# Attention and GELU MLP on one core: seven products of blocks instead of eight for the first product of the last two tiles

## The chip, the cores and the metric

The kernel runs on one core of a Trainium2 chip. The metric is the device time of one execution in microseconds (us), the median of several runs. The engines of the core that matter here are TensorE (PE in the profile; its weight loads are shown apart, as PEld), VectorE (DVE), ScalarE (ACT), GpSimd (POOL), and SyncE (SP), whose queue issues every DMA of this kernel.

## What is computed

For 8 batches of 8 heads with 576 positions of 64 numbers: causal attention in a window of 128 positions with a linear bias for each head, and then an MLP with GELU on the 4608 rows of 512 that it leaves. Cut to what matters:

```python
scores = scale * q @ k.T                      # for each batch and head
scores = where(mask, scores + bias, -1e9)     # 0 <= i - j < 128, bias = -slope * (i - j)
attn = softmax(scores) @ v
x = attn as [4608, 512]
h = x @ w_in                                  # 512 -> 2048
g = 0.5 * h * (1 + erf(h / sqrt(2)))
out = g @ w_out                               # 2048 -> 512
```

## The kernel before

Every large operand of a product is held as two fp16 parts, a high one and a low one, after a scaling by a power of two, and a product of two such operands takes three matmuls: high by high, low by high, high by low. The parts are made by ACT or POOL (high) and DVE (low, `low_part`, L146).

The 4608 rows of x are worked in nine tiles of 512 (t = 0 to 8). A tile has two products. The first, `mlp_in` (L588 to L620), takes 16 blocks fc of 128 columns of w_in; each is 4 parts of the contraction by 3 terms, 12 matmuls of 512 columns (L595), so 192 in a tile. ACT takes each block out of PSUM with Gelu (L618) into a tile of the tag `ob` (three buffers), POOL makes the high part (L619), DVE the low part (L146). The second, `mlp_out` (L638), takes 4 blocks tb of 128 rows, 16 fc by 3 terms each, again 192 matmuls of 512 columns (L653); DVE or ACT takes the result out (L663, L661) and SP stores it (L664). Both products share four PSUM banks (tag `mm`). The weights of w_in stay in eight pairs `wi[n]`, [128, 2 parts, 4 parts of the contraction, 256 columns].

Attention of batch b = t + 1 is issued in the middle of tile t, for t up to 6, so tiles 7 and 8 hold the MLP alone. A batch has four units hp. Of each: the scores on PE (L410, tile `sc`, PSUM tag `att`), taken out by DVE with the bias (L432, tile `s`), a maximum on DVE (L502, `nmax`), exponentials on ACT (L505), the split into `e_main` by POOL (L514) and DVE (L146), two transposes by DMA into `et` (L517: EVEN, five groups, then ODD, four), and the product with v on PE (`weigh`, L554, tile `av`), taken out into the rows of x of the next tiles (L567 on ACT, then L146). Beside them run the steps for the next batch: `load_v`, `stat_v` (L214 is its maximum over all of v, `stv`), `split_v` (`vbuf`), `load_qk`, `split_qk` (`qbuf`, `kbuf`).

The program writes these in the order of steps in the loop at L767: step 0 to 15 issues `mlp_in`, step 16 to 31 four fc of `mlp_out`, scores at `SCORES_AT`, weighings at `WEIGH_AT`. From that a scheduler with a timeline of its own and priorities sets the order of each engine; an engine then runs its list strictly in order. So an instruction that waits holds back all behind it on its engine, and a DMA that waits holds back all behind it on SP. The exponentials are given a higher priority (`EXP_AHEAD`).

## Time and profile before

| | us |
|---|---|
| median of 3 runs (lowest to highest) | 954.64 (951.97 to 955.38) |
| the profiled execution | 956.14 |
| its span in the trace | 954.3 |
| PE busy | 920.4 |
| DVE busy | 626.1 |
| ACT busy | 493.4 |
| POOL busy | 214.5 |
| mean granted clock of TensorE | 0.984 of full speed |

The profiled execution took 956.14 us, of which the trace covers a span of 954.3; the 1.8 us between them lie outside the instructions. A sum made on the trace is a sum against 956.14, which is 1.5 us above the median of the runs. [...]

### The profile page before, as it was taken

What the parts mean: (1) busy time and instruction counts of PE and PEld (TensorE: products, weight loads), DVE (VectorE), ACT (ScalarE), POOL (GpSimd) and SP (SyncE); (2) the same over time, 40 slices, a digit from 0 to 9 for tenths busy, and PEclk for the clock granted to TensorE, in tenths of its full rate; (3) what the DMA queues carried; (4) which work ended last, traced back from release to release, by engine and by line L of the source; (5) the groups of instructions that cost most, each with busy time, mean ns of one, the idle gap of its engine ahead of it and who ended that gap; (6) DMA issues with size and microseconds to landing.
All of it is one profiled execution on the core that took longest, in us unless ns stands there. A gap on an engine that the chain in (4) does not pass through costs nothing.

```text
span 954.3 us, 17680 instructions
## 1 busy us (share of the span) xinstructions
PE 920.4 (96%) x7068; PEld 448.8 (47%) x7068; DVE 626.1 (66%) x1270; ACT 493.4 (52%) x1071; POOL 214.5 (22%) x444
## 2 busy tenths in 40 slices
...
DVE  6799989689786877497768876777566722201200
...
DMA packets 172450, 91.18 MB, mean 96 GB/s; under 512 B 132560, under 2 KB 153168, under 8 KB 172240
## 3 DMA queue, kind: packets, MB, share of 16 engines
...
q14 instruction: 27, 0.22, 0.1%
...
## 4 chain that ended last, share of the span: by engine, by line
PE 54%; DMA 2%; DVE 2%; ACT 2%; issue 1%; SPq 0%; POOL 0%; DVEq 0%
PE o L653 26%; PE h L595 22%; PE av L554 3%; PE sc L410 2%; DMA v<-vp 1%; DMA q<-qp 1%; DVE stv L214 1%; DMA et<-e_main 1%; ACT vbuf L332 1%; DVE vbuf L146 0%; ACT s L505 0%; DVE kbuf L146 0%; ACT L618 0%; ACT L505 0%; SPq L305 0%
## 5 line engine op out<-in xcount | busy, mean ns | idle before, releaser
L595 PE MATMUL h<-x,wi 128*128 128x512 f16 x1728 | 385.0, 381 | 6.6 <-ACT g L618 3.0
L653 PE MATMUL o<-wo,g 128*128 128x512 f16 x1224 | 276.4, 379 | 0.2 <-DVE wo L146 0.2
L595 PEld LDWEIGHTS <-wi 128*128 128x128 f16 x1728 | 166.8, 98 | 209.2 <-issue 12.3
L653 PEld LDWEIGHTS <-g 128*128 128x128 f16 x1632 | 155.0, 98 | 186.6 <-issue 2.3
L146 DVE SCALAR_TENSOR_TENSOR g<-g,sg,g 128x512 f16<-128x512 f32 (+1 forms) x144 | 114.1, 805 | 92.7 <-POOL g L619 91.5
L619 POOL TENSOR_SCALAR g<-g,sg 128x512 f16<-128x512 f32 x128 | 100.4, 788 | 316.7 <-ACT g L618 312.4
L505 ACT ACTIVATE s<-s,nmax 128x192 f32<-128x192 f32 x252 | 111.2, 442 | 103.2 <-DVE nmax L502 103.0
L618 ACT ACTIVATE g<-h,gs 128x512 f32<-128x512 f32 x128 | 85.9, 687 | 135.8 <-PE h L595 111.0
L146 DVE SCALAR_TENSOR_TENSOR e_main<-s,z,e_main 128x192 f16<-128x192 f32 x252 | 107.3, 468 | 15.0 <-POOL e_main L514 10.2
L514 POOL TENSOR_SCALAR e_main<-s,z 128x192 f16<-128x192 f32 x180 | 87.1, 503 | 84.9 <-ACT s L505 29.3
L653 PE MATMUL o<-wo_first,g 128*128 128x512 f16 x408 | 94.6, 382 | 2.8 <-DMA wo_first<-wo 2.8
L410 PE MATMUL sc<-kbuf,qbuf 64*64 64x192 f16 (+1 forms) x1656 | 75.6, 264 | 10.8 <-DMA kbuf<-kp 4.5
L432 DVE SCALAR_TENSOR_TENSOR s<-sc,cs,bias_h 128x384 f32<-128x384 f32 x112 | 63.7, 606 | 14.3 <-PE sc L410 14.1
L567 ACT ACTIVATE x<-av,cx 128x448 f16<-128x448 f32 (+6 forms) x52 | 23.7, 474 | 72.8 <-PE av L554 72.6
L437 POOL MEMSET s<- 64x128 f32 (+1 forms) x112 | 19.2, 172 | 185.8 <-DVE s L432 167.3
L502 DVE TENSOR_REDUCE nmax<-s 128x5 f32<-128x960 f32 (+1 forms) x56 | 58.4, 1044 | 2.1
L661 ACT ACTIVATE ob<-o,so 128x512 f32<-128x512 f32 x17 | 11.5, 678 | 91.2 <-PE o L653 91.1
L410 PEld LDWEIGHTS <-qbuf 64*64 64x64 f16 x1512 | 36.1, 106 | 43.0 <-issue 40.2
L663 DVE TENSOR_SCALAR ob<-o,so 128x512 f32<-128x512 f32 x17 | 12.6, 744 | 60.0 <-PE o L653 60.0
L554 PEld LDWEIGHTS <-vbuf 128*64 128x64 f16 x1680 | 43.3, 115 | 12.4 <-issue 11.5
L554 PE MATMUL av<-et,vbuf 128*64 128x128 f16 (+1 forms) x1680 | 46.4, 216 | 2.6 <-DMA et<-e_main 2.6
L505 ACT ACTIVATION_READ_ACCUMULATOR s<-s,nmax 128x1 f32 x252 | 47.1, 187 | 0.0
...
## 6 DMA issues: line engine op xcount, KB each, us to landing
...
out<-ob SPq DMA_DIRECT2D x36, 256.0 KB, 2.1
...
```

The source lines that it names most:

```text
L146: nc.vector.scalar_tensor_tensor(out=dst, in0=src, scalar=scale, in1=high, op0=ALU.mult, op1=ALU.subtract)
L410: nc.tensor.matmul(ps[bank][o, n, 0:W], a, m, start=(i == 0), stop=(i == len(terms) - 1 and b > 0), skip_group_check=True,)
L432: nc.vector.scalar_tensor_tensor(out=s[:, bank[0] : bank[0] + k, :], in0=ps[bank][:, 0:k, 0:W], scalar=cs, in1=bias.broadcast_to([P, k, W] ...
L502: nc.vector.tensor_reduce(out=nmax[:, r], in_=s[:, r], axis=AX.X, op=ALU.max, negate=True)
L505: nc.scalar.activation(s[:, i, :], s[:, i, :], AF.Exp, bias=nmax[:, i : i + 1], accum_out=z[:, i : i + 1])
L514: nc.gpsimd.tensor_scalar(e[:, i, 0, c], s[:, i], z[:, i : i + 1], 1.0, op0=ALU.mult, op1=ALU.mult)
L554: nc.tensor.matmul(av[r, (j - blocks[0]) * QB : (j - blocks[0] + len(js)) * QB], v32s[b][:, hp, kb, r] if b < EXACT else vbuf[:, vi, hp, k ...
L567: nc.scalar.activation(x[:, 0], av[:, :n], AF.Copy, scale=c)
L595: nc.tensor.matmul(ph, wi[n][:, a, cc, k * P : (k + 1) * P], x[:, cc, b, :], start=(i == 0), stop=(i == 3 * NCC - 1),)
L618: nc.scalar.activation(g32, ph, AF.Gelu, scale=gsc[t, n])
L619: nc.gpsimd.tensor_scalar(g[:, r, 0], g32, gsg[t, n], 1.0, op0=ALU.mult, op1=ALU.mult)
L653: nc.tensor.matmul(o, both[:, a, c], wo[n][:, b, k, :], start=(fc == first and i == 0), stop=(fc == last and i == 2),)
```

## The change

**Tiles 7 and 8 (`FAST = 7`).** The first product is made in four groups d of 512 columns of w_in (two pairs `wi`). In each, the weights are four blocks (256 columns by half of the contraction) and x is four blocks (half of the contraction by 256 rows), and the eight products of blocks are replaced by seven (p1 to p7) of sums of blocks. Each is 2 by 2 by 3 = 12 matmuls of 256 columns, so a group has 84 and a tile 336. Two PSUM banks, u and v, gather them; ACT copies u to SBUF three times in a group (s1, s2, s3), DVE adds v to these copies, and four results of [128, 512] go through Gelu on ACT, a high part on ACT (before: POOL) and a low part on DVE. That is 11 ACT and 7 DVE instructions in a group. `p4` and `p3` of the last group are issued in the second product.

**Sums of weights.** Four sums of blocks (T1 to T4) are needed for each d. They are made once, in 16 parts of [128, 512] (`sums_of_weights`): two additions of 256 on DVE, four dependent ones of 128, a cast on ACT, a difference of 512 on DVE, and four DMAs that store them to DRAM in pieces of 256 bytes. Three parts each stand beside the second products of tiles 2 to 5, four beside that of tile 6. T1 is then loaded over a block of `wi[2d + 1]` that is no longer needed (four DMAs); T2 to T4 are loaded for each d as they are needed, 256 KB each, into one buffer each (`stream`), the next one behind the product that reads the last.

**Sums of x.** `sums_of_x` makes the sums of blocks of x: six DVE instructions (two of 1024, four of 256) and a cast of 1024 on ACT, twice for a tile: for tile 7 in tile 6, behind the weighings of units 1 and 3, for tile 8 in the second product of tile 7.

**Smaller things.** One power of two is taken for both weights of a pair, which adds one small DVE instruction for each of four calls at the start; scales move by one bit to leave room for the sums; the first two pairs of tile 0's `mlp_in` lose their higher priority.

```diff
-        pow2_of_words(pww[:, r], stat)
-        inverse(sww[:, r], pww[:, r])
+        nc.vector.tensor_tensor(out=stat[:, 0:1], in0=stat[:, 0:1], in1=stat[:, 1:2], op=ALU.max)
+        pow2_of_words(pww[:, r], stat[:, 0:1].broadcast_to([P, len(ns)]))
+        inverse(sww[:, r], pww[:, r], 12)
...
+    stored = dram.tile([4, NWP // 2, P, 2, 2, 256], F16, name="stored")
+    S2, S3, S4, S1 = range(4)
+    T2, T3, T4, T1 = range(4)
...
+    def sums_of_weights(d, i, half):
+        c = slice(half * NH, (half + 1) * NH)
+        r, st = (pool.tile([P, TT], F32, tag="ob", name=f"{n}{d}_{i}_{half}", bufs=3) for n in ("tr", "ts"))
+        r = r.rearrange("p (m c f) -> p m c f", m=2, c=2)
+        st = st.bitcast(F16).rearrange("p (a s f) -> p a s f", a=2, s=4)
+        for m in range(2):
+            w = wi[2 * d + m]
+            nc.vector.tensor_tensor(
+                out=r[:, m], in0=w[:, 0, 2 * i : 2 * i + 2, c], in1=w[:, 1, 2 * i : 2 * i + 2, c], op=ALU.add
+            )
+        b11, b21, b12, b22 = r[:, 0, 0], r[:, 0, 1], r[:, 1, 0], r[:, 1, 1]
+        nc.vector.tensor_tensor(out=b11, in0=b12, in1=b11, op=ALU.subtract)
+        nc.vector.tensor_tensor(out=b12, in0=b22, in1=b12, op=ALU.subtract)
+        nc.vector.tensor_tensor(out=b22, in0=b22, in1=b11, op=ALU.subtract)
+        nc.vector.tensor_tensor(out=b21, in0=b21, in1=b22, op=ALU.subtract)
+        flat = r.rearrange("p m c f -> p (m c f)")
+        hi, lo = (st[:, a].rearrange("p s f -> p (s f)") for a in range(2))
+        nc.scalar.copy(hi, flat)
+        nc.vector.tensor_tensor(out=lo, in0=flat, in1=hi, op=ALU.subtract)
+        for n, k in ((T1, 0), (T2, 3), (T3, 2), (T4, 1)):
+            nc.sync.dma_start(stored[n, d, :, :, i, c], st[:, :, k])
+    def sums_in_place():
+        for d in range(NWP // 2):
+            nc.sync.dma_start(wi[2 * d + 1][:, :, 0 : NCC : 2], stored[T1, d])
+        for n in (T2, T3, T4):
+            stream(n, 0)
+    def stream(n, d):
+        nc.sync.dma_start(streams[n], stored[n, d])
...
+    def sums_of_x(t, i):
+        x = x_tile(t)[:, 2 * i : 2 * i + 2]
+        r = pool.tile([P, 2, TT], F32, tag="v32", name=f"r{t}_{i}", bufs=1)
+        nc.vector.tensor_tensor(out=r, in0=x[:, :, 0], in1=x[:, :, 1], op=ALU.add)
+        a11, a21, a12, a22 = r[:, 0, 0:HT], r[:, 0, HT:TT], r[:, 1, 0:HT], r[:, 1, HT:TT]
+        nc.vector.tensor_tensor(out=a22, in0=a21, in1=a22, op=ALU.add)
+        nc.vector.tensor_tensor(out=a21, in0=a11, in1=a21, op=ALU.subtract)
+        nc.vector.tensor_tensor(out=a11, in0=a22, in1=a11, op=ALU.subtract)
+        nc.vector.tensor_tensor(out=a12, in0=a12, in1=a11, op=ALU.subtract)
+        flat = r.rearrange("p c n -> p (c n)")
+        hi, lo = (sums[i][:, a].rearrange("p s f -> p (s f)") for a in range(2))
+        nc.scalar.copy(hi, flat)
+        nc.vector.tensor_tensor(out=lo, in0=flat, in1=hi, op=ALU.subtract)
...
+    class Seven:
+        def __init__(self, t, d):
+            self.t, self.d, self.x = t, d, x_tile(t)
+            self.lo, self.hi = wi[2 * d], wi[2 * d + 1]
...
+        def add(self, ps, w, m, first):
+            n = 0
+            for k in range(2):
+                for i in range(2):
+                    for a, b in ((0, 0), (1, 0), (0, 1)):
+                        nc.tensor.matmul(
+                            ps[:, k * HT : (k + 1) * HT], w(a, i)[:, k * P : (k + 1) * P], m(b, i),
+                            start=first and n == 0, stop=True, skip_group_check=True,
+                        )
+                        n += 1
+        def out(self, hi, tok, src, room=None):
+            t, d = self.t, self.d
+            room = src if room is None else room
+            nc.scalar.activation(room, src, AF.Gelu, scale=gsc[t, 2 * d])
+            g = g_of[t, d][:, 2 * hi : 2 * hi + 2, :, tok * HT : (tok + 1) * HT]
+            v = room.rearrange("p (k f) -> p k f", k=2)
+            nc.scalar.activation(g[:, :, 0], v, AF.Copy, scale=gsg[t, 2 * d])
+            low_part(g[:, :, 1], v, gsg[t, 2 * d], g[:, :, 0])
+        def p1(self):
+            self.u = self.bank("u")
+            self.add(self.u, lambda a, i: self.lo[:, a, 2 * i], lambda b, i: self.x[:, 2 * i, b, 0:HT], True)
+            self.s1 = self.room("s1")
+            nc.scalar.copy(self.s1, self.u)
+        def p2(self):
+            self.v = self.bank("v")
+            self.add(self.v, lambda a, i: self.lo[:, a, 2 * i + 1], lambda b, i: self.x[:, 2 * i + 1, b, 0:HT], True)
+            nc.vector.tensor_tensor(out=self.s1, in0=self.v, in1=self.s1, op=ALU.add)
+            self.out(0, 0, self.s1)
+        def p6(self):
+            self.add(self.u, lambda a, i: streams[T2][:, a, i], lambda b, i: sums[i][:, b, S2], False)
+            self.s2 = held2[self.d % 2]
+            nc.scalar.copy(self.s2, self.u)
+        def p5(self):
+            self.add(self.v, lambda a, i: self.hi[:, a, 2 * i], lambda b, i: sums[i][:, b, S1], True)
+        def p7(self):
+            self.add(self.u, lambda a, i: streams[T3][:, a, i], lambda b, i: sums[i][:, b, S3], False)
+            s3 = self.room("s3")
+            nc.scalar.copy(s3, self.u)
+            nc.vector.tensor_tensor(out=s3, in0=self.v, in1=s3, op=ALU.add)
+            self.out(1, 1, s3)
+        def p4(self):
+            self.add(self.u, lambda a, i: streams[T4][:, a, i], lambda b, i: self.x[:, 2 * i + 1, b, HT:TT], False)
+            self.out(0, 1, self.u, self.room("s4"))
+        def p3(self):
+            self.add(self.v, lambda a, i: self.hi[:, a, 2 * i + 1], lambda b, i: sums[i][:, b, S4], False)
+            nc.vector.tensor_tensor(out=self.s2, in0=self.v, in1=self.s2, op=ALU.add)
+            self.out(1, 0, self.s2)
+    def stream_next(t, n, d):
+        if d < NWP // 2 - 1:
+            stream(n, d + 1)
+        elif t + 1 < NTILE:
+            stream(n, 0)
+    def seven_steps(t):
+        if not held2:
+            both = pool.tile([P, NG * 2, P], F32, tag="et0", name="held2", bufs=1).rearrange("p n f -> p (n f)")
+            held2.extend(both[:, n * TT : (n + 1) * TT] for n in range(2))
+        q = [Seven(t, d) for d in range(NWP // 2)]
+        order = []
+        for d in range(len(q)):
+            order += [q[d].p1, q[d].p2]
+            if d:
+                order += [(q[d - 1].p4, T4, d - 1)]
+            order += [(q[d].p6, T2, d)]
+            if d:
+                order += [q[d - 1].p3]
+            order += [q[d].p5, (q[d].p7, T3, d)]
+        order += [(q[-1].p4, T4, len(q) - 1), q[-1].p3]
+        def run(job):
+            if isinstance(job, tuple):
+                job[0]()
+                stream_next(t, *job[1:])
+            else:
+                job()
+        n = len(order) - 2
+        steps = [[order[k], order[k + 1]] for k in range(0, n, 2)]
+        return [lambda jobs=jobs: [run(j) for j in jobs] for jobs in steps], [lambda j=j: run(j) for j in order[n:]]
     units = {}
...
     for n in range(NWP):
         if n == 2:
             load_qk(1)
-        with tc.high_priority(400):
+        with tc.high_priority(400 if n >= 2 else 0):
...
+    PARTS_AT = {2: (19, 23, 27), 3: (19, 23, 27), 4: (19, 23, 27), 5: (19, 23, 27), 6: (17, 19, 21, 23)}
+    parts = [(d, i, half) for d in range(NWP // 2) for i in range(2) for half in range(2)]
...
+        fast = t >= FAST
+        if fast:
+            first, rest = seven_steps(t)
+        else:
+            first, rest = [lambda fc=fc: mlp_in(t, fc) for fc in range(NFC)], []
+        if t + 1 == FAST:
+            room_for_sums()
+        for step in range(len(first) + NFC):
+            if step < len(first):
+                first[step]()
             else:
-                tb, q = divmod(step - NFC, 4)
+                tb, q = divmod(step - len(first), 4)
                 for fc in range(4 * q, 4 * q + 4):
                     mlp_out(t, tb, fc)
+                if tb == 0 and q < len(rest):
+                    rest[q]()
+            if fast and t + 1 < NTILE and step in (len(first) + 1, len(first) + 4):
+                sums_of_x(t + 1, int(step > len(first) + 1))
+            if step in PARTS_AT.get(t, ()):
+                sums_of_weights(*parts.pop(0))
+                if not parts:
+                    sums_in_place()
             if b >= B:
                 continue
...
             if step in weigh_at:
-                weigh(unit(b, weigh_at.index(step)))
+                hp = weigh_at.index(step)
+                weigh(unit(b, hp))
+                if hp % 2 and t + 1 == FAST:
+                    sums_of_x(FAST, hp // 2)
```

Lines of the new kernel are shifted: L146 is L149 there, L214 is L217, L432 is L437, L502 is L507, L517 is L522.

The steps set a new order. DVE at the start of tile 3 (`stv` is the maximum over the next batch's v, `sc_0` and `s_0` belong to unit 0, `g` to the first product), before:

```order
L146 SCALAR_TENSOR_TENSOR g_0_4662<-g_3_0_4663,sg_0_4645,g_0_4662 128x512
L146 SCALAR_TENSOR_TENSOR g_0_4662<-g_3_1_4680,sg_0_4645,g_0_4662 128x512
L214 TENSOR_REDUCE stv_4888<-v_5_4686 128x1
L432 SCALAR_TENSOR_TENSOR s_0_4712<-sc_0_0_4713,cs_4402,bias_h 128x384
L432 SCALAR_TENSOR_TENSOR s_0_4712<-sc_0_2_4714,cs_4402,bias_h 128x384
L146 SCALAR_TENSOR_TENSOR g_0_4662<-g_3_2_4708,sg_0_4645,g_0_4662 128x512
L116 COPY quarters<-stv_4888 32x1 x2
L432 SCALAR_TENSOR_TENSOR s_0_4712<-sc_0_4_4760,cs_4402,bias_p 128x192
L116 COPY quarters<-stv_4888 32x1 x2
L146 SCALAR_TENSOR_TENSOR g_0_4662<-g_3_3_4756,sg_0_4645,g_0_4662 128x512
L502 TENSOR_REDUCE nmax_0_4816<-s_0_4712 128x5
```

and after:

```order
L149 SCALAR_TENSOR_TENSOR g_0_4711<-g_3_0_4712,sg_0_4694,g_0_4711 128x512
L149 SCALAR_TENSOR_TENSOR g_0_4711<-g_3_1_4729,sg_0_4694,g_0_4711 128x512
L437 SCALAR_TENSOR_TENSOR s_0_4761<-sc_0_0_4762,cs_4437,bias_h 128x384
L437 SCALAR_TENSOR_TENSOR s_0_4761<-sc_0_2_4763,cs_4437,bias_h 128x384
L149 SCALAR_TENSOR_TENSOR g_0_4711<-g_3_2_4757,sg_0_4694,g_0_4711 128x512
L217 TENSOR_REDUCE stv_4937<-v_5_4735 128x1
L437 SCALAR_TENSOR_TENSOR s_0_4761<-sc_0_4_4809,cs_4437,bias_p 128x192
L149 SCALAR_TENSOR_TENSOR g_0_4711<-g_3_3_4805,sg_0_4694,g_0_4711 128x512
L119 COPY quarters<-stv_4937 32x1 x4
L507 TENSOR_REDUCE nmax_0_4865<-s_0_4761 128x5
```

The maximum `stv`, which waited for the load of v ahead of the first two evictions `s_0`, stands behind them and behind one more low part of g, but still ahead of the third eviction and of `nmax`.

SP at the end of tile 6 (`et_3` is unit 3, the transpose of 20 groups EVEN, that of 16 ODD), before:

```order
L517 DMA_TRANSPOSE et_2_9065<-e_main 128x16x128
L664 DMA out<-ob_1_9270 128x512
L517 DMA_TRANSPOSE et_3_9305<-e_main 128x20x128
L517 DMA_TRANSPOSE et_3_9305<-e_main 128x16x128
L664 DMA out<-ob_2_9456 128x512
L664 DMA out<-ob_3_9574 128x512
```

and after:

```order
L710 DMA stored<-ts_0_1_9310 256x1x128 x4
L720 DMA room_8572<-stored 128x1024 x3
L710 DMA stored<-ts_1_0_9423 256x1x128 x4
L669 DMA out<-ob_1_9499 128x512
L522 DMA_TRANSPOSE et_3_9555<-e_main 128x20x128
L710 DMA stored<-ts_1_1_9503 256x1x128 x4
L715 DMA wi_773<-stored 128x4x256
L522 DMA_TRANSPOSE et_3_9555<-e_main 128x16x128
L669 DMA out<-ob_2_9706 128x512
L669 DMA out<-ob_3_9832 128x512
```

Between the two transposes of unit 3 there now stand the four stores of the last part and the load of T1 into `wi`, which waits for the store of T1; before them stand the stores of two more parts and three loads.

ACT at the start of tile 7, before:

```order
L618 ACT_TABLE_LOAD
L618 ACTIVATE g_7_0_9597<-h_0_9583,gs_0_9577 128x512
L618 ACTIVATE g_7_1_9614<-h_1_9601,gs_0_9577 128x512
L618 ACTIVATE g_7_2_9631<-h_2_9618,gs_0_9577 128x512
L618 ACTIVATE g_7_3_9648<-h_3_9635,gs_0_9577 128x512
```

and after (`s_0` and `held` are rooms for copies of u and results):

```order
L778 COPY s_0_9859<-u_0_9846 128x512
L768 ACT_TABLE_LOAD
L768 ACTIVATE s_0_9859<-s_0_9859,gs_0_9835 128x512
L771 ACTIVATE g_0_9842<-s_0_9859,sg_0_9837 128x2x256
L789 COPY held_9841<-u_0_9846 128x512
L797 COPY s_0_9916<-u_0_9846 128x512
L778 COPY s_1_9936<-u_1_9923 128x512
L768 ACTIVATE s_0_9916<-s_0_9916,gs_0_9835 128x512
L768 ACTIVATE s_1_9936<-s_1_9936,gs_0_9835 128x512
L768 ACTIVATE s_0_9967<-u_0_9846,gs_0_9835 128x512
L771 ACTIVATE g_0_9842<-s_0_9916,sg_0_9837 128x2x256
L771 ACTIVATE g_1_9843<-s_1_9936,sg_0_9837 128x2x256
```

Where ACT did one Gelu for each 12 matmuls of 512 columns, it now alternates copies of u, Gelus and high parts, 11 for each 84 matmuls of 256 columns.

## Rows read from the trace of the kernel before

**Rows 1.** View: the head of the page: busy time and share of the span of each engine; then one line of the view in 40 equal slices of 23.9 us (busy tenths of DVE).

```profile
PE 920.4 (96%) x7068; PEld 448.8 (47%) x7068; DVE 626.1 (66%) x1270; ACT 493.4 (52%) x1071; POOL 214.5 (22%) x444
...
DVE  6799989689786877497768876777566722201200
```

**Rows 2.** View: the chain of work that ended last, its end: start, us, engine, tile, line and count.

```profile
784.79 41.44 PE h L595 x192
826.23 41.44 PE o L653 x192
867.67 41.44 PE h L595 x192
```

**Rows 3.** View: busy time by stretch: stretch, its length, busy us and count of PE, PEld, DVE, ACT and POOL, clock granted, DMA share, GB/s. 735 to 768 lies in tile 6, 785 to 826 is the first product of tile 7 and 826 to 868 its second.

```profile
735.00:768.00 33.00, 33.00 (x350) 16.37 (x349) 23.49 (x55) 15.95 (x53) 12.62 (x31) 1.00 0.48 94
...
785.00:826.00 41.00, 41.00 (x192) 18.58 (x190) 11.49 (x16) 12.10 (x17) 10.51 (x15) 1.00 0.02 7
826.00:868.00 42.00, 42.00 (x197) 19.04 (x195) 2.25 (x3) 1.67 (x3) 0.69 (x1) 1.00 0.05 19
```

**Rows 4.** View: timeline of PE in the first 45 us: matmuls of 384 columns back to back, and the row that starts when the fourth is through.

```profile
42.05 0.81 PE L485 MATMUL tp<-bias_h,adders 128*128 128x384 bf16 x4
42.70 1.04 PE L491 MATMUL tp<-ident,vbuf 128*128 128x128 f32 x8
```

**Rows 5.** View: groups of instructions by line and form over the whole span: busy us, mean ns of one, idle before.

```profile
L618 ACT ACTIVATE g<-h,gs 128x512 f32<-128x512 f32 x128 | 85.9, 687 | 135.8 <-PE h L595 111.0 <-DVE g L146 22.2 <-issue 1.6
...
L193 DVE SCALAR_TENSOR_TENSOR zi<-zi,raw 128x1024 int32<-128x1024 int32 x8 | 9.7, 1219 | 0.0
...
L493 ACT COPY et<-tp 128x512 f32<-128x512 f32 x16 | 9.0, 614 | 1.6 <-PE tp L491 1.6
L204 ACT ACTIVATE wi<-zi,sww 128x1024 f16<-128x1024 f32 x8 | 8.7, 1139 | 2.4 <-DVE sww L141 2.4
...
L485 PEld LDWEIGHTS <-adders 128*128 128x128 bf16 x40 | 4.2, 111 | 4.2 <-issue 2.9
...
L146 DVE SCALAR_TENSOR_TENSOR x<-av,cx,x 128x256 f16<-128x256 f32 x8 | 3.8, 476 | 1.4 <-ACT x L567 1.4
...
L146 DVE SCALAR_TENSOR_TENSOR x<-av,cxl,x 128x512 f16<-128x512 f32 x4 | 3.0, 748 | 1.8 <-ACT x L567 1.8
...
L567 ACT ACTIVATE x<-av,scv 128x512 f16<-128x512 f32 x4 | 2.9, 714 | 3.1 <-PE av L554 3.1
...
L146 DVE SCALAR_TENSOR_TENSOR x<-av,cx,x 128x128 f16<-128x128 f32 x8 | 2.7, 343 | 6.7 <-ACT x L567 6.6
```

**Rows 6.** View: timeline of PE where tiles 2 to 4 begin or end and PE waited: start, us, operation, count and, in brackets, idle time before it and what ended that.

```profile
320.32 4.03 PE L595 MATMUL h<-x,wi 128*128 128x512 f16 x11 [2.42 <-ACT g L618]
...
389.34 0.85 PE L554 MATMUL av<-et,vbuf 128*64 128x128 f16 x29 [0.69 <-DMA et<-e_main]
...
408.29 0.81 PE L410 MATMUL sc<-kbuf,qbuf 64*64 64x192 f16 x15 [1.71 <-DVE s L432]
...
521.09 3.18 PE L595 MATMUL h<-x,wi 128*128 128x512 f16 x14 [0.61 <-ACT g L618]
```

**Rows 7.** View: busy time by stretch around these waits; the clock granted is the column behind POOL.

```profile
408.00:412.00 4.00, 3.71 (x23) 1.51 (x23) 3.88 (x10) 0.08 (x1) 1.97 (x4) 0.59 0.00 0
412.00:416.00 4.00, 4.00 (x20) 1.86 (x19) 3.93 (x13) 3.40 (x11) 0.29 (x2) 0.98 0.00 0
...
388.00:392.00 4.00, 3.31 (x76) 2.16 (x74) 2.54 (x2) 1.74 (x2) 0.00 (x0) 1.00 0.38 112
521.00:525.00 4.00, 3.91 (x19) 1.78 (x19) 3.44 (x10) 1.89 (x4) 3.87 (x7) 1.00 0.77 147
```

**Rows 8.** View: timeline of DVE at the start of tile 3.

```profile
404.90 2.82 DVE L214 TENSOR_REDUCE stv<-v 128x1 f32<-128x2560 f32 x1 [4.62 <-DMA v<-vp]
407.63 1.13 DVE L432 SCALAR_TENSOR_TENSOR s<-sc,cs,bias_h 128x384 f32<-128x384 f32 x2
...
411.40 1.15 DVE L502 TENSOR_REDUCE nmax<-s 128x5 f32<-128x960 f32 x1
```

**Rows 9.** View: timeline of ACT at the start of tile 3.

```profile
412.58 0.46 ACT L505 ACTIVATE s<-s,nmax 128x192 f32<-128x192 f32 x1 [4.50 <-DVE nmax L502]
...
421.37 1.84 ACT L618 ACTIVATE g<-h,gs 128x512 f32<-128x512 f32 x3
```

**Rows 10.** View: timeline of the SP queue: the load of v at the end of tile 2, and the last two transposes of tile 6.

```profile
396.11 2.10 SPq L305 DMA_DIRECT2D v<-vp  x4
...
765.34 5.12 SPq L517 DMA_TRANSPOSE et<-e_main  x2
```

**Rows 11.** View: timeline of PE at the end of tile 6: the last product with v.

```profile
775.24 5.34 PE L653 MATMUL o<-wo,g 128*128 128x512 f16 x24
780.52 1.57 PE L554 MATMUL av<-et,vbuf 128*64 128x64 f16 x60
```

**Rows 12.** View: the tile et from 760 to 785 us: issue and landing of the same two transposes.

```profile
L517 SPq DMA_TRANSPOSE et<-e_main x2: 2072/2536/3001, 765.3 to 768.4; - x2
...
DMA to landing us min/median/max: 4.4/4.7/5.0
```

**Rows 13.** View: DMA issues over the whole span: count, KB of one, median us from issue to landing.

```profile
out<-ob SPq DMA_DIRECT2D x36, 256.0 KB, 2.1
...
et<-e_main SPq DMA_TRANSPOSE x56, 4.8
```

More of the change, by code (lines that the diff above doesn't have):

```diff
@@ L28 @@
 TT = 512
+FAST = 7
+HT = TT // 2
 NTILE = NT // TT
@@ L321, in stat_v @@
             sx[b] = small([P, 1], f"sx{b}", 3, tag="sx")
[L322 removed]
+            inverse(sx[b], pwx[b], 12 if b >= FAST else 13)
         for t in (b - 1, b):
```

30 lines of the change are left out of this document (21 added, 9 removed).

## Prediction

> **What bounds the kernel now.** I read the head of the page first: PE is busy 96% of the span, DVE 66%, ACT 52% [rows 1]. The chain of waits says the same closer: in its last four steps it runs through PE alone, 192 matmuls in each product, 41.44 us each [rows 2], so 41.44/192 = 215.8 ns for a matmul of 512 columns. Tiles 7 and 8 are thus pure PE time, and what is taken from PE there comes off the end, provided that the other engines keep up. They have room: in the first product of tile 7 DVE is busy 11.5 and ACT 12.1 of 41 us, and in its second 2.3 and 1.7 of 42 [rows 3]. The stretches with attention are the other case. The slices show DVE at 6 to 8 tenths there [rows 1], and the timeline of PE shows where it already waits: 2.42 us at 320, 0.69 at 389, 1.71 at 408, 0.61 at 521 [rows 6]. [...] So the reader has two accounts to keep: columns saved in tiles 7 and 8, and DVE, ACT and SP work put into tiles 2 to 6, where waits of a microsecond or two already stand.
>
> **The columns saved.** A tile's first product goes from 192 matmuls of 512 columns to 336 of 256. The trace has no row of 256 fp16 columns with weights of 128 by 128. The nearest of 384 columns: four start at 42.05 and the next work at 42.70 [rows 4], 162.5 ns each. Through 162.5 at 384 and 215.8 at 512 a straight line gives 109.2 ns at 256. 336 x 109.2 = 36.7 us, 4.7 less than 41.44, and 9.5 for two tiles. One bound is half of 215.8, 107.9 ns: 36.3 us, 10.4 for both. The other is the weight load, one for each matmul, at 111 ns in the nearest row [rows 5]: 37.3 us, 8.3 for both. I take 9.5, since the straight line has two rows.
>
> ACT has 11 instructions for a group whose matmuls take 84 x 109.2 = 9.17 us: 3 copies of 0.614, 4 Gelus of 0.687, 4 high parts of 0.714 [rows 5], 7.4 us. DVE has 7 of about 0.75 [rows 5], 5.2 us. Both fit, ACT with 19% to spare. The order puts the copies of u ahead of other results, so a bank is released early. I allow 0.5 us for the start of tile 7 and the passages between the products, from nothing to 1.5. The loads of T2 to T4, 256 KB each, have the time of about six products of blocks, 7.9 us, against 2.1 for a store of that size [rows 13]; POOL loses its share of this work, which nobody waits for.
>
> **The sums of weights.** A part has on DVE two instructions of 256, four of 128 and one of 512. Two-operand instructions of these sizes took 0.476, 0.343 and 0.748 [rows 5]: 2 x 0.476 + 4 x 0.343 + 0.748 = 3.07 us, and 16 parts 49 us. `sums_of_x` takes 2 x 1.219 + 4 x 0.476 = 4.3 us and a cast of 1.14 on ACT [rows 5]. None of this is on the chain by itself; what counts is who stands behind it. [...]
>
> *End of tiles 2 to 5.* Three parts, 9.2 us, stand among the low parts of unit 3, so its ODD transpose starts later, and four stores stand ahead of it on SP. The scheduler also lets the last product with v start some 12 matmuls, 2.6 us, later. I take it that these cancel and that the wait of 0.69 at 389 [rows 6] goes: -0.7, between -0.7 and +1.5.
>
> *Start of tile 3.* In the row before, `stv` waited 4.62 us for v, and the evictions `s` queued behind its 2.82 us [rows 8]; PE's scores waited for them, 1.71 us, and 1.7 more went with the clock. The new order puts `stv` behind the first two evictions, and this wait goes: -3.4. But `stv` is still ahead of `nmax`, and v lands later: `vbuf`, which frees its buffer, is behind the parts on DVE (3.07 each), and the four issues of the load, 2.1 us on SP [rows 10], behind stores. Say 2.5 us. What was `nmax` at 411.40 [rows 8], exponentials at 412.58 and the Gelus held back behind them at 421.37 [rows 9] then comes 2 to 3 later, while PE arrives 3.4 earlier, and the first product waits for its PSUM banks. Estimated, 0.4 to 3.8 us of the 3.4 comes back; I take 1.9, so -1.5 net.
>
> *Start of tiles 4 and 5.* The same delay meets a wait of 0.61 for a Gelu that is there already [rows 6] and a tile 5 that had none: +2.0 (0 to 3.7, the top with a clock loss of 1.7) and +0.8 (0 to 2.5).
>
> *Tile 6.* Four parts and one `sums_of_x` are 4 x 3.07 + 4.3 = 16.6 us of new DVE work around a stretch in which DVE idles 33.00 - 23.49 = 9.5 [rows 3]: 7.1 over. The last ODD transpose was issued at 768.4 (765.34 and the 3.0 of the EVEN one), landed by 772.8, and was wanted at 780.52 [rows 10 to 12]: 7.7 in hand. Take 7.1 and then the stores, the load of `wi` and its wait for a store to land, all ahead of it in SP's new order: 4 x 0.52 [rows 10] + 2.1 [rows 13] = 4.2. So 3.6 us too late at worst, some of which earlier waits absorb. Evictions of units 2 and 3 behind parts and sums make waits of 0.5 to 1.5 each before it. I take +3.5 in all; the ends are 0 and 7, with one clock loss in the latter.
>
> [...]
>
> *Tiles 0 and 1.* The priority change moves a few matmuls past each other, and one small DVE instruction is added four times. No row prices this: 0, with 2.5 either way.
>
> **The sum.** -9.5 + 0.5 - 0.7 - 1.5 + 2.0 + 0.8 + 3.5 = -4.9 us. Against the profiled execution, 956.14, that is 951.2; the median of runs is 1.5 lower, 954.64, and gives 949.7. I write 950.
>
> **Rivals.** (1) *The new work is hidden.* DVE's waits for others take up the parts, as its idle of 9.5 us in tile 6 allows in large part, and the waits at 389 and 408 go: -9.5 - 0.7 - 3.4 = -13.6, or 941 from the median; with a microsecond or two given back 943. For: DVE idles a third of the span. Against: it idles for its releasers, not when the parts come, and each list is strictly in order.
> (2) *The gain is given back almost whole.* All debts at their upper middle: 1.0 + 3.8 - 3.4 + 3.7 + 2.5 + 5.5 against 9.5: +3.6 at worst, centre near 955.
> (3) *Slower.* The waits in tiles 3 to 6 grow past the size at which the clock falls. Seen are a fall behind 1.71 and none behind 0.69 [rows 6, 7], so it decides between those. Five waits (starts of tiles 4 and 5, two evictions and the transpose in tile 6) of 2 us with 1.7 each are 18.5, plus 0.4 for tile 3, less 13.6: +5.3, 960. Against: five must be that long.
> (4) *The seven products don't run at their columns' rate.* If ACT's instructions took 0.84 us each in place of 0.68, 11 would be 9.2 and PE would wait in every group; at 10.3 us a group the saving is nil and (2) and (3) follow. For: results come in bursts. Against: the first product had ACT at 12.1 of 41 [rows 3].
>
> **How the numbers follow.** A chance of 0.42 for the forecast (946 to 953), 0.18 for (1) (941 to 946), 0.22 for (2) (953 to 958), 0.18 for (3) and (4) on the slow side. The range leaves out half of that last and the low tail of (1): 942 to 960. A difference of 0.5%, 4.8 us, is about what a measurement of this kernel can tell from no change: faster is under 949.9, which takes (1) and somewhat over half of the forecast, 0.43; slower is over 959.4, 0.18; the rest is 0.39.
>
> **What would show it.** In the new trace: first products of tiles 7 and 8 in 36.3 to 37.5 us without idle time of PE; no wait for `s` at the start of tile 3 and the clock at 1.0 there; waits for ACT's Gelu of 2 to 3 us a few microseconds into tiles 3 to 5; waits for evictions and for `et` in the second product of tile 6, 2 to 5 us together. I am wrong if PE waits inside the seven products, if the waits in tiles 2 to 6 are all under a microsecond, or if tiles 0 and 1 have moved by more than 2.5.

## The result and the profile after

The changed kernel took 960.32 us (median of 6 runs) against 954.01: a ratio of 1.0074, with a 95% interval of 1.0045 to 1.0102. On another chip it was 962.07 against 951.58, 1.0106 (1.0083 to 1.0129). The ratios differ from those of the medians beside them by up to 0.2%. Left out of all times is one slow run each of the changed kernel on that other chip (1168.72 us, granted clock 0.753) and of the run with the parts on GpSimd (2731.65 us). The change makes the kernel slower by 6 to 10 us, where 4.9 us faster was forecast; the time lies just outside the range. It is the time of rival (3), 960.

The head of the page after, as [rows 1]:

```profile
span 959.9 us, 18628 instructions
...
PE 911.4 (95%) x7356; PEld 473.3 (49%) x7356; DVE 687.2 (72%) x1435; ACT 539.6 (56%) x1147; POOL 196.3 (20%) x412
```

PE is busy 9 us less than before, and the span is 5.6 us longer: time without work on PE has grown. The end of the chain of waits, as [rows 2] (start, us, engine, tile, line, count):

```profile
798.28 1.31 PE u L757 x12
...
877.23 1.31 PE u L757 x12
...
921.43 34.76 PE o L658 x161
```

A product of blocks takes 1.31 us, 109 ns for a matmul, as worked out. From the start of tile 7 to that of tile 8 it is 877.23 - 798.28 = 78.95 us, before 867.67 - 784.79 = 82.88 [rows 2]; tile 8 takes 921.43 + 34.76 - 877.23 = 78.96. So 3.9 us are saved in each, 7.9 together. But tile 7 starts 13.5 us later than it did. The timeline of PE shows where this went, as [rows 6] (in brackets the idle time before the row and what ended it):

```profile
319.23 0.87 PE L600 MATMUL h<-x,wi 128*128 128x512 f16 x2 [2.33 <-ACT g L623]
...
391.26 0.91 PE L559 MATMUL av<-et,vbuf 128*64 128x128 f16 x32 [0.92 <-DVE stq L217]
...
421.69 0.93 PE L600 MATMUL h<-x,wi 128*128 128x512 f16 x2 [2.42 <-ACT g L623]
...
493.57 0.64 PE L559 MATMUL av<-et,vbuf 128*64 128x128 f16 x16 [0.69 <-DMA et<-e_main]
...
523.63 0.59 PE L600 MATMUL h<-x,wi 128*128 128x512 f16 x2 [2.43 <-ACT g L623]
...
596.18 1.02 PE L559 MATMUL av<-et,vbuf 128*64 128x128 f16 x40 [1.44 <-DVE stq L217]
...
625.99 0.86 PE L600 MATMUL h<-x,wi 128*128 128x512 f16 x3 [2.00 <-ACT g L623]
...
792.42 0.76 PE L559 MATMUL av<-et,vbuf 128*64 128x64 f16 x24 [2.07 <-DMA et<-e_main]
...
808.12 1.14 PE L757 MATMUL u<-x,room 128*128 128x256 f16 x9 [0.67 <-ACT s L797]
```

and busy time by stretch behind four of these waits, as [rows 7] (the clock is the column behind POOL):

```profile
421.60:425.60 4.00, 3.91 (x11) 1.48 (x11) 3.30 (x12) 1.88 (x4) 3.87 (x7) 0.57 1.01 125
523.60:527.60 4.00, 3.97 (x11) 1.50 (x11) 3.46 (x13) 1.82 (x3) 3.92 (x7) 0.58 0.86 164
625.90:629.90 4.00, 3.91 (x11) 1.50 (x11) 3.29 (x14) 1.88 (x4) 3.87 (x7) 0.59 0.86 164
792.40:796.40 4.00, 3.98 (x61) 2.29 (x62) 2.28 (x5) 0.69 (x1) 0.00 (x0) 0.68 0.05 19
```

At the starts of tiles 3, 4 and 5 (421, 523, 625) PE waits 2.0 to 2.4 us for a Gelu, at the ends of tiles 2, 3 and 4 (391, 493, 596) for unit 3's `et` (twice put down to `stq` on DVE, which ends in the same moment; in a second trace of this kernel, below, these two are put down to `et` as well), and in tile 6 2.07 for it. Behind each of the three starts the clock is at 0.57 to 0.59 over 4 us, behind the last at 0.68 and then 0.89 over two such stretches. In stretches of 0.2 us it reads 0.50 there, half clock, for 3.4 us in one piece, and 1.00 on both sides. The 24 matmuls of 512 columns behind each of the three starts take 7.03 us; at the start of tile 5 in the second trace of this kernel, where the clock stays at 1.00, they take 5.34: 1.7 us lost each time. Before, the start of tile 3 had this [rows 7], 0.50 from 408.7 to 412.1; that of tile 2 (319, in [rows 6] 320) has it in both traces, 0.50 from 319.4 to 322.8 after and from 320.0 to 323.4 before. The wait in tile 7, 0.67 at 808, is for ACT's copy of u; tile 8 has the same one.

Why the Gelu is late, by the SP queue from the end of tile 4. In the kernel before:

```profile
573.78 5.53 SPq L517 DMA_TRANSPOSE et<-e_main  x1
579.37 0.57 SPq L347 DMA_DIRECT2D k<-kp  x1
583.06 2.98 SPq L517 DMA_TRANSPOSE et<-e_main  x1
...
594.52 2.10 SPq L305 DMA_DIRECT2D v<-vp  x4
```

and after:

```profile
577.98 5.19 SPq L522 DMA_TRANSPOSE et<-e_main  x1
583.26 3.40 SPq L710 DMA_DIRECT2D stored<-ts  x4
586.71 0.61 SPq L352 DMA_DIRECT2D k<-kp  x1
...
588.11 5.91 SPq L522 DMA_TRANSPOSE et<-e_main  x1
...
602.84 2.10 SPq L310 DMA_DIRECT2D v<-vp  x4
```

From the issue of the EVEN transpose to that of k it is 5.6 us before and 8.7 after: the four stores stand between, 3.4 us of SP's time. To the load of v it is 20.7 before and 24.9 after, 4.1 us more. In between stand the ODD transpose, which now starts 1.4 us behind the issue of k instead of 3.7 and holds SP for 5.91 instead of 2.98 us, and DVE, which maximizes k when it lands and only then makes the low part of v (`vbuf`), which frees the room that v is loaded into. At the end of tile 2, before ([rows 10] has the load of v, at 396.11) and after:

```profile
374.33 5.78 SPq L517 DMA_TRANSPOSE et<-e_main  x1
```

```profile
373.58 5.36 SPq L522 DMA_TRANSPOSE et<-e_main  x1
...
398.04 2.99 SPq L310 DMA_DIRECT2D v<-vp  x4
```

Here it is 21.8 before and 24.5 after, so v is only 2.7 us later; at the end of tile 3 it is 3.2. What is behind the load of v at the end of tile 4, after:

```profile
593.49 2.55 DVE L217 TENSOR_REDUCE stq<-k 128x1 f32<-128x2304 f32 x1 [4.22 <-DMA k<-kp]
...
599.93 2.88 DVE L149 SCALAR_TENSOR_TENSOR vbuf<-v,scv,vbuf 128x2560 f16<-128x2560 f32 x1 [2.29 <-ACT vbuf L337]
...
609.58 2.82 DVE L217 TENSOR_REDUCE stv<-v 128x1 f32<-128x2560 f32 x1 [2.63 <-DMA v<-vp]
...
613.93 1.15 DVE L507 TENSOR_REDUCE nmax<-s 128x5 f32<-128x960 f32 x1
```

and on ACT, where `s` is exponentiated and the three Gelus at 625 release the banks:

```profile
615.17 1.28 ACT L510 ACT_TABLE_LOAD   x1 [4.13 <-DVE square L120]
...
625.25 1.84 ACT L623 ACTIVATE g<-h,gs 128x512 f32<-128x512 f32 x3
```

The exponentials wait for `nmax` (`square`, which the row names, ends 0.05 us behind it), and here the load of their table waits with them, 1.28 us more; before, at the same place, it ran at 605.32, ahead of that wait.

### The profile page after: what moved, and what is told of

Its sections match the earlier page's. It is cut to its first block, busy times and chain, and to the rows that moved or that the text cites. A ratio compares the mean times of both kernels' runs of the same rounds, so it can differ in the third digit from the quotient of the medians.

```text
span 959.9 us, 18628 instructions
## 1 busy us (share of the span) xinstructions
PE 911.4 (95%) x7356; PEld 473.3 (49%) x7356; DVE 687.2 (72%) x1435; ACT 539.6 (56%) x1147; POOL 196.3 (20%) x412
## 4 chain that ended last, share of the span: by engine, by line
PE 55%; DVE 12%; DMA 8%; ACT 7%; issue 3%; SPq 2%; POOL 0%; DVEq 0%; ACTq 0%; POOLq 0%
PE o L658 26%; PE h L600 15%; PE u L757 4%; PE v L757 3%; PE av L559 3%; DMA et<-e_main 3%; PE sc L415 3%; DMA v<-vp 3%; ACT s L510 2%; DVE e_main L149 2%; DVE vbuf L149 1%; DVE stv L217 1%; DMA k<-kp 1%; DVE nmax L507 1%; DVE s L437 1%
## 5 line engine op out<-in xcount | busy, mean ns | idle before, releaser
L600 PE MATMUL h<-x,wi 128*128 128x512 f16 x1344 | 306.4, 385 | 14.2 <-ACT g L623 9.2
L600 PEld LDWEIGHTS <-wi 128*128 128x128 f16 x1344 | 129.8, 99 | 174.4 <-issue 25.8
L624 POOL TENSOR_SCALAR g<-g,sg 128x512 f16<-128x512 f32 x96 | 78.6, 824 | 213.8 <-ACT g L623 205.2
L149 DVE SCALAR_TENSOR_TENSOR e_main<-s,z,e_main 128x192 f16<-128x192 f32 x252 | 107.8, 470 | 8.8 <-POOL e_main L519 4.5
L623 ACT ACTIVATE g<-h,gs 128x512 f32<-128x512 f32 x96 | 63.7, 686 | 80.9 <-PE h L600 54.6
L519 POOL TENSOR_SCALAR e_main<-s,z 128x192 f16<-128x192 f32 x180 | 89.1, 513 | 89.2 <-issue 45.1
L149 DVE SCALAR_TENSOR_TENSOR g<-g,sg,g 128x512 f16<-128x512 f32 (+1 forms) x112 | 87.2, 795 | 23.3 <-POOL g L624 21.0
L437 DVE SCALAR_TENSOR_TENSOR s<-sc,cs,bias_h 128x384 f32<-128x384 f32 x112 | 63.8, 608 | 6.5 <-PE sc L415 6.3
L507 DVE TENSOR_REDUCE nmax<-s 128x5 f32<-128x960 f32 (+1 forms) x56 | 58.4, 1043 | 2.3 <-POOL s L442 0.2
L559 PE MATMUL av<-et,vbuf 128*64 128x128 f16 (+1 forms) x1680 | 44.2, 210 | 11.6 <-DMA et<-e_main 9.2
L559 PEld LDWEIGHTS <-vbuf 128*64 128x64 f16 x1680 | 41.1, 111 | 22.0 <-issue 11.9
L707 ACT CAST ts<-tr 128x512 f16<-128x512 f32 x16 | 9.8, 614 | 57.6 <-DVE tr L704 53.6
```

The costliest lines, as they stand in the source:

```text
L149: nc.vector.scalar_tensor_tensor(out=dst, in0=src, scalar=scale, in1=high, op0=ALU.mult, op1=ALU.subtract)
L437: nc.vector.scalar_tensor_tensor(out=s[:, bank[0] : bank[0] + k, :], in0=ps[bank][:, 0:k, 0:W], scalar=cs, in1=bias.broadcast_to([P, k, W] ...
L507: nc.vector.tensor_reduce(out=nmax[:, r], in_=s[:, r], axis=AX.X, op=ALU.max, negate=True)
L519: nc.gpsimd.tensor_scalar(e[:, i, 0, c], s[:, i], z[:, i : i + 1], 1.0, op0=ALU.mult, op1=ALU.mult)
L559: nc.tensor.matmul(av[r, (j - blocks[0]) * QB : (j - blocks[0] + len(js)) * QB], v32s[b][:, hp, kb, r] if b < EXACT else vbuf[:, vi, hp, k ...
L600: nc.tensor.matmul(ph, wi[n][:, a, cc, k * P : (k + 1) * P], x[:, cc, b, :], start=(i == 0), stop=(i == 3 * NCC - 1),)
```

## The experiments

Theory **SP**: the stores on SP's queue, ahead of k and of the transposes, make v late. Theory **DVE**: the parts' instructions, ahead of the low parts of `e_main` and v, do. Ratios are to the kernel before on the same chip; the experiments ran on four chips, so they are compared with each other by these ratios.

**Without the parts.** The edit of the first run, and that of the second instead of it (both keep the loads of T1, at step 23 of tile 6):

```diff
-            if step in PARTS_AT.get(t, ()):
-                sums_of_weights(*parts.pop(0))
...
+            if t == 6 and step in (5, 6, 7, 8):
+                for n in (T1, T2, T3, T4):
+                    nc.sync.dma_start(stored[n, step - 5], wi[2 * (step - 5)][:, :, 0 : NCC : 2])
...
+            if t == 6 and step == 5:      # second run; every d then reads stored[n, 0]
+                for n in (T1, T2, T3, T4):
+                    nc.sync.dma_start(stored[n, 0], x_tile(6)[:, 2:4, :, HT:TT])
```

> The 16 parts (DVE sums, casts, stores) are left out; the changed kernel's seven products stay, fed with raw blocks of w_in that 16 DMAs store to DRAM early in tile 6 (so the output is not the reference's). Sums of x, loads of T1 to T4 and the priority change stay. Both theories (stores on SP's queue, or work on DVE, make v late) put the whole loss of tiles 2 to 6 on the parts: the waits of 2.4, 2.4 and 2.0 us for a Gelu at the starts of tiles 3 to 5 go back to 0 to 0.6, half clock behind them goes, and the time is 954.0 - 7.9 (what the two seven-product tiles save in the trace of after) + 0 to 2 = 946 to 948. If it stays above 952, the parts are not the cause and the seven products or the priority change are.

> As the run without parts, but what stands in DRAM for the sums is one set of blocks of x, stored by four DMAs at the start of tile 6, since the 16 stores of raw blocks had been moved by the scheduler into tile 0 and changed the order of tiles 0 and 1 (the output is not the reference's). Tiles 0 and 1 are now in the order of the changed kernel. If the parts are the whole loss: 7.9 us from the seven products and 3.3 from the start of tile 3, 10 to 12 us under the kernel before on the same chip (940 to 942 if that is 952). If it stays within 5 us of before, tiles 0 and 1 in the new order lose what is missing.

First: 949.72 against 951.89, 0.9974 (0.9960 to 0.9987), where 946 to 948 was expected; tiles 0 and 1 had been reordered by the stores (the wait near 320 ends at 324.42 in its trace), so its time tells little. Second: 945.49 against 952.32, 0.9948 (0.9925 to 0.9972), 5.0 us less by the ratio and 6.8 by the medians. PE's timeline at the start of tile 2 in the second, and the start of tile 7 in its chain of waits:

```profile
319.96 0.85 PE L600 MATMUL h<-x,wi 128*128 128x512 f16 x2 [2.41 <-ACT g L623]
```

```profile
780.03 1.31 PE u L757 x12
```

From the one to the other it is 460.1 us, in the two traces of the changed kernel 479.1 and 477.7, in those of the kernel before 464.5 and 460.1. So the parts are the loss of tiles 2 to 6: sums of x and the loads of T1 stayed and cost nothing that shows there. The 10 to 12 us expected are not there. A good part of the gap is in the reference: of the 3.4 us at the start of tile 3 in the trace of before, another execution lacks 2.7 (below).

**The parts without the seven products** (tiles 7 and 8 as before):

```diff
-        if fast:
+        if False:
```

> The parts, stores, sums of x and the T1 loads stay, but tiles 7 and 8 use the old first product of 192 matmuls of 512 columns (T1 overwrites blocks that it reads, so the output is not the reference's). By both theories the loss of tiles 2 to 6 stays whole and the saving is gone: 960.3 + 7.9 = 968, between 966 and 970. A time under 964 would say that the seven products lose time that the trace's tiles 7 and 8 do not show.

966.24 against 951.89: 1.0144 (1.0109 to 1.0180), 14 us for the parts and their company. The level, 966, was as expected. From the two ratios of the changed kernel, 1.0074 and 1.0106, the seven products take 6.7 or 3.6 us off, each known to some 4 us; the first allows the 7.9 of the trace, the second almost. In the trace of this run tiles 7 and 8 take 82.88 us each, as before, and the stretch from 320 to tile 7 is 478.8, as in the changed kernel; what the traces differ by beyond that lies in tiles 0 and 1.

**One store for each part, and the parts on GpSimd.**

```diff
-        for n, k in ((T1, 0), (T2, 3), (T3, 2), (T4, 1)):
-            nc.sync.dma_start(stored[n, d, :, :, i, c], st[:, :, k])
+        nc.sync.dma_start(stored[:, d, :, :, i, c].rearrange("n p a f -> p a n f"), st)
```

So that one DMA can write all four, T1 to T4 are numbered in the order in which they stand in `st`. On GpSimd, all `nc.vector` of `sums_of_weights` become `nc.gpsimd`.

> Each part is stored by one DMA of 1024 pieces of 256 bytes in place of four DMAs of 256 pieces; nothing else changes, and DVE's order stays that of after. Theory SP (the stores stand ahead of the load of k and of the ODD transpose, so k, stq, vbuf, the load of v, stv and the exponentials come late): 3 x 0.6 us less per part on SP, k some 2 us and v some 3 to 4 us earlier, waits at the starts of tiles 3 to 5 fall from 2.0 to 2.4 to under 1 us with no half clock behind them: 950 to 954. Theory DVE (the parts' 3 us each on VectorE delay the low parts of e_main and vbuf): 958 to 961, waits as in after.

> The eight DVE instructions of each part run on GpSimd instead; casts on ACT and the four stores on SP stay. Theory SP: the stores stand where they stood and come no earlier, so the waits stay and the time is 958 to 963. Theory DVE: DVE's order is that of the kernel before at these places, the waits at the starts of tiles 3 to 5 shrink to under 1 us and the time is 949 to 953.

> Parts on GpSimd and one store for each. If SP's queue and DVE's time each delay v by their own share (one store took 10.9 us off the stretch of tiles 3 to 6, GpSimd 7.8 of the 20.1 that the parts cost there), the two together leave 1 to 3 us of it: 7 to 9 us under before (943 to 945 if that is 952). If it is one delay seen from two sides, the result is that of one store alone, 950 to 952.

One store: 951.49 against 951.89, 1.0004 (0.9991 to 1.0016). On GpSimd: 956.15, 1.0048 (1.0030 to 1.0066). Both: 949.37 against 952.32, 0.9974 (0.9957 to 0.9991). Against the changed kernel's 1.0106 these are 9.7, 5.5 and 12.6 us less, against its 1.0074 3 us less than that each. From the wait near 320 to the start of tile 7 (in each up to 1.7 of half clock behind that wait):

| trace | us |
|---|---|
| changed kernel, two traces | 479.1, 477.7 |
| parts on GpSimd | 471.2 |
| one store | 466.6 |
| both | 464.7 |
| no parts | 460.1 |

One store lies where theory SP had it. GpSimd lies between the forecasts of the two theories, and both together, 3 us under one store alone, between those of two shares and of one delay. So both theories hold, SP's with the larger share, and one without the other explains less than the two. The timeline of SP with one store, at the place shown above:

```profile
574.71 5.25 SPq L522 DMA_TRANSPOSE et<-e_main  x1
580.01 0.61 SPq L710 DMA_DIRECT2D stored<-ts  x1
580.66 0.67 SPq L352 DMA_DIRECT2D k<-kp  x1
...
597.85 2.10 SPq L310 DMA_DIRECT2D v<-vp  x4
```

k is now 5.95 us behind the transpose, v 23.1. PE's waits, and the clock behind them, with one store:

```profile
421.47 0.95 PE L600 MATMUL h<-x,wi 128*128 128x512 f16 x3 [2.29 <-ACT g L623]
...
521.84 0.38 PE L600 MATMUL h<-x,wi 128*128 128x512 f16 x1 [1.71 <-ACT g L623]
...
620.82 0.38 PE L600 MATMUL h<-x,wi 128*128 128x512 f16 x1 [1.62 <-ACT g L623]
```

```profile
421.40:425.40 4.00, 3.93 (x11) 1.47 (x11) 3.30 (x12) 1.86 (x4) 3.89 (x7) 0.58 0.94 121
521.80:525.80 4.00, 3.96 (x19) 1.82 (x19) 3.30 (x12) 1.83 (x3) 3.92 (x7) 1.00 0.86 164
620.80:624.80 4.00, 3.98 (x19) 1.85 (x19) 3.31 (x14) 1.81 (x3) 3.94 (x7) 1.00 0.87 166
```

The waits at 521 and 620 are only 0.7 and 0.4 us shorter, but no half clock follows them, which is 3.4 us more. The wait for `et` in tile 6 is gone, and its half clock with it, 3.8 us. Of the waits at the ends of tiles 2 to 4, 3.0 us together, one of 0.61 is left. These make some 11 of the 12.5 us between the two traces in the table above. "Under 1 us" was wrong; "950 to 954" right. With the parts on GpSimd the waits at the starts of tiles 3 to 5 are 2.37, 1.48 and 1.20 us, only the first with half clock behind it.

**The parts earlier** (one store, on DVE):

```diff
-    PARTS_AT = {2: (19, 23, 27), 3: (19, 23, 27), 4: (19, 23, 27), 5: (19, 23, 27), 6: (17, 19, 21, 23)}
+    PARTS_AT = {2: (10, 14, 19), 3: (10, 14, 19), 4: (10, 14, 19), 5: (10, 14, 19), 6: (10, 14, 17, 19)}
```

> One store for each part, on DVE, and the parts at steps 10, 14 and 19 of tiles 2 to 5 (10, 14, 17, 19 of tile 6) instead of 19, 23, 27, so that nothing of them stands between unit 3 and the load of v. If what matters is that the parts stand ahead of the end of the tile, where the chain k, stq, vbuf, v, stv, exponentials runs: waits at the starts of tiles 3 to 5 under 1 us, 4 to 8 us under before (944 to 948). If DVE's total time matters (49 us more wherever it stands), PE waits for Gelu or evictions in the middle of the tiles instead: 950 to 954.

958.62 against 952.32, 1.0079 (1.0050 to 1.0107): slower than with the parts at the end of the tile, and beyond what either reading expected. The waits have moved; PE's timeline:

```profile
432.48 0.70 PE L559 MATMUL av<-et,vbuf 128*64 128x128 f16 x21 [2.36 <-DVE s L437]
...
534.06 1.15 PE L559 MATMUL av<-et,vbuf 128*64 128x64 f16 x43 [2.32 <-DVE s L437]
...
634.61 0.67 PE L559 MATMUL av<-et,vbuf 128*64 128x128 f16 x11 [2.60 <-DVE s L437]
```

DVE's timeline ahead of the first:

```profile
431.20 0.69 DVE L709 TENSOR_TENSOR ts<-tr,ts 128x512 f16<-128x512 f32 x1 [0.74 <-ACT ts L708]
431.81 1.14 DVE L437 SCALAR_TENSOR_TENSOR s<-sc,cs,bias_h 128x384 f32<-128x384 f32 x2
```

The starts of tiles 3 and 5 no longer wait, and that of tile 4 waits 0.61. Now the product with v and the scores wait for banks that the evictions `s` release, and these stand behind a part, its wait of 0.74 for ACT's cast included. Behind the first and the third of the waits the clock is at 0.61 and 0.57 over 4 us. At neither of the two placements tried is there a place of 3 us on DVE in the tiles with attention that nothing waits for.

**The priority of tile 0.** One store with `tc.high_priority(400)` for all pairs again:

> The run with one store, with the higher priority of 400 back on the first two pairs of tile 0. By the traces the new order of tiles 0 and 1 gains 1.1 to 3.3 us by the start of tile 3: 1 to 3 us slower than one store, 952 to 955. If the priority does nothing, within 1 us of it.

952.92 against 952.32, 1.0012 (0.9989 to 1.0035), the interval overlapping that of one store: not told apart by time. In the trace the wait near 320 ends at 324.30, with one store at 321.25.

**One tile of seven products, the parts beside tile 7.**

```diff
-FAST = 7
+FAST = 8
...
+    PARTS_AT = {7: (4, 6, 8, 10, 12, 14, 16, 17, 18, 19, 21, 22, 23, 24, 25, 26)}
...
+            if t + 1 == FAST and step in (18, 20):
+                sums_of_x(FAST, int(step > 18))
```

and in the last run, with the sums of x at steps 0 and 1, `PARTS_AT = {7: (2, 4, 6, 8, 10, 12, 14, 15, 16, 17, 18, 19, 20, 21, 22, 23)}`; one store in each.

> Seven products in tile 8 alone, and all 16 parts, each with one store, and the sums of x moved into tile 7, where DVE is busy 11.5 of 41 us and 2.3 of 42 in the kernel before. Tiles 2 to 6 then hold nothing new. If the loss comes only from where the parts stand: the 3.9 us that tile 8 saves in the trace of after stay, and the waits at the starts of tiles 3 to 5 are those of before (none over 1 us but the one at 320): 3 to 6 us under before (946 to 949 if that is 952). If the parts cost wherever they stand, PE waits in tile 7 and the time is that of before or above.

> The same with the priority of 400 back on the first two pairs of tile 0. If the new order of tiles 0 and 1 is worth its 1 to 3 us of the traces: 1 to 3 us slower than the run with one such tile. If it is only the scatter of single executions: within 1 us.

> As the run with one tile of seven products, with the sums of x at steps 0 and 1 of tile 7 and the parts ended by step 23, so that their rooms (the tag ob) are free when tile 8 begins. If the waits of 0.84 and 3.50 us with a half clock of 1.7 behind them in tile 8 came from the parts still holding these rooms: they go, tile 8 saves 3.9, and the time is 4 to 6 us under before (946 to 948 if that is 952). If seven products start badly wherever the parts end, 952 to 954 as before.

First: 953.01 against 951.58, 1.0012 (1.0000 to 1.0025); with the old priority 954.82, 1.0039 (1.0018 to 1.0061), the intervals overlapping a little. PE's timeline of the first at the start of tile 8, and ACT's copy that it waits for:

```profile
871.28 1.09 PE L757 MATMUL u<-room,room 128*128 128x256 f16 x6 [3.50 <-ACT s L778]
```

```profile
870.65 0.58 ACT L778 COPY s<-u 128x512 f32<-128x512 f32 x1 [3.30 <-DMA out<-ob]
```

The copies' rooms share a tag with the parts' and the results', and wait for a store. The stretch from 320 to tile 7 is 460.7 us, as without parts, but tile 8 takes 85.4 us and saves nothing. In the last run the copies don't wait for it:

```profile
870.23 1.03 PE L757 MATMUL u<-x,room 128*128 128x256 f16 x8 [0.67 <-ACT s L797]
```

949.76 against 952.17: 0.9974 (0.9957 to 0.9991). With one tile of seven products and its sums where DVE has time, the saving holds: 2.4 us under before by the medians, less than the 4 to 6 expected, and 3.9 in tile 8 of the trace. This version and the one with GpSimd and one store both beat both kernels.

**Both kernels again.**

> The kernel before, unchanged, for a second trace on another chip. If the clock loss of 1.7 us behind the wait at 408 and the long stretch at half clock near 170 belong to every execution, both stand in this trace too and its time is about 956; if they depend on the execution, one or both are missing and the time is 950 to 954. Rivals alike expect the wait of 1.7 us for s at the start of tile 3 itself.

> The changed kernel, unchanged, on the chip of the other runs, so that one store and GpSimd stand beside it in one place: 5 to 8 us above before (957 to 960 if that is 952); waits of 2.0 to 2.4 us for Gelu at the starts of tiles 3, 4 and 5 with half clock behind each, as in the first trace. If half clock is missing behind some, the loss is 1.7 us smaller for each.

Before: 952.19 us. Its timeline of PE at the start of tile 3, and the clock there:

```profile
406.12 0.68 PE L410 MATMUL sc<-kbuf,qbuf 64*64 64x192 f16 x15 [0.66 <-DVE s L432]
```

```profile
406.00:410.00 4.00, 3.88 (x31) 1.97 (x31) 3.88 (x10) 0.96 (x1) 1.97 (x4) 1.00 0.00 0
```

The wait is 0.66, not 1.71 [rows 6], and the clock stays at 1.0: of the 3.4 us that the prediction credited to this place this execution has 0.7. The stretch at half clock near 170 stands in this trace too (granted clock 0.82 from 170 to 175, 0.50 from there to 180), if shorter: in the first trace it is 0.50 from 169.8 to 180.0. After: 962.07, above the 957 to 960 expected, with waits of 2.43, 2.28 and 1.81 at the starts of tiles 3 to 5 and 2.25 in tile 6, the third without half clock.

## Why the prediction was wrong

By its own terms, in the two first traces:

| term | forecast | measured |
|---|---|---|
| columns of tiles 7 and 8, with their passages | -9.0 | -7.9 |
| ends of tiles 2 to 5, waits for `et` | -0.7 | +2.4 (0.92 - 0.69, 0.69, 1.44) |
| start of tile 3 | -1.5 | +0.7 (2.42 - 1.71, half clock in both) |
| start of tile 4 | +2.0 | +3.5 (2.43 - 0.61 + 1.7) |
| start of tile 5 | +0.8 | +3.7 (2.00 + 1.7) |
| tile 6 | +3.5 | +4.4 (2.07 + 1.7, and 0.6: two groups of scores took 0.91 and 1.09 instead of 0.69) |
| tiles 0 and 1, as the rest of 13.5 | 0 | -1.2 (319.23 - 320.32 at the start of tile 2) |
| sum | -4.9 | +5.6, as the spans |

- **The step that failed** is the price of the new waits at the starts of tiles 3 to 5 and in tile 6: the middles 1.9, 2.0, 0.8 and 3.5 hold no loss of clock, which was charged to upper ends alone. Yet the prediction expected waits of "2 to 3 us" there and had seen the clock fall behind 1.71. The waits themselves came out near their sum, 8.9 us (2.42, 2.43 - 0.61, 2.00, 2.07 + 0.6) against 8.2. Half clock behind four of them took 1.7 more each, 6.8 of the 10.5 us between forecast and measurement. It is not certain behind such a wait: in the second trace of the changed kernel it follows three of the four.
- **The ends of the tiles** are the next step that failed, 3.1 us: the later product with v was to cancel the later transpose. It did not. With one store one wait of 0.61 is left of the three, so the stores made most of them; that the ODD transpose also holds SP longer, 5.05 to 5.91 us against 2.88 to 3.35 before at these ends, is seen, but not tested alone.
- **How late v comes**, "say 2.5 us", was right in kind and near in size: 2.7, 3.2 and 4.1 us at the ends of tiles 2, 3 and 4. The path was told in part only: the estimate had the stores on SP only ahead of the load of v, but they stand ahead of k as well, and k is ahead of v by way of DVE; and the load of the table put another 1.3 on the exponentials.
- **The columns** were right: 109 ns. The saving is 1.1 less than the forecast, all passages included; one wait of 0.67 for ACT stands in each tile, which the prediction had named as a sign of being wrong.
- **The credit at the start of tile 3** was not there in the second execution of the kernel before. The first has it as the sum took it: 1.71 of waiting, and half of the 3.4 us at 0.50, 1.7.
- **Tile 6** was right in kind and nearly in size, but by other terms than its own: the wait for `et` is 2.07, and its half clock, left to the upper end, makes up what the evictions did not take. One store removes the wait.
- **Rival (3)** had the price right, 960, partly by luck. It has five waits of 2 us with half clock; there were four, three of them where it said (tiles 4 and 5, the transpose in tile 6), and none for evictions. Its sum also takes 0.4 as coming back at tile 3, where the prediction's own upper end was 3.8 and 4.1 came back, and counts the ends of the tiles as a gain of 0.7.
- **The range** held every debt near its middle and left out half of a case with 18% chance. These debts have one cause, the parts, so they come high together, and their upper ends were the case to weigh.
- **The pieces of 256 bytes.** DMA issues of the run with one store, with the median us to landing:

```profile
out<-ob SPq DMA_DIRECT2D x36, 256.0 KB, 2.2
...
stored<-ts SPq DMA_DIRECT2D x16, 256.0 KB, 3.2
```

3.2 us for a store of 256 KB in pieces of 256 bytes, 2.2 in long ones: slower by 1.0. The sum of tile 6 took the 2.1 of a long store [rows 13] for the one ahead of the load of `wi`; in the changed kernel that is one of 64 KB in pieces of 256 bytes, 2.0 in the median.

- **A part** took 2 x 0.415 + 4 x 0.30 + 0.681 = 2.7 us on DVE (after, instructions of 256, 128 and 512), not 3.07.

What stays open: whether tile 0's priority does anything (both runs with the old one are slower, by 0.8 and 2.6 us, within their intervals), how much of the 7.9 us of the seven products a median shows, and what decides whether half clock follows a wait of some 2 us.
